# Four small reorderings in a fused attention and MLP kernel: memory read-out ahead, weight loads split, w_down scaling in segment 0, other LN times

## The chip, the cores and the metric

The kernel runs on one core of one Trainium2 chip. The metric is the device time of one execution in microseconds. A ratio is the mean time of one kernel's fast runs over the mean of the other's fast runs of the same rounds, so it isn't quite the ratio of the medians that are quoted beside it. "Faster" and "same" are meant at 2%.

## The reference

One block on 2048 tokens of width 448: an adaptive layer norm (LN) with modulation from `c`, attention in four segments of 512 tokens with a running memory `M`, a residual, a second adaptive LN, and a gated MLP.

```
mod = (silu(c) @ w_mod)                    # six rows: sa, ca, ga, sb, cb, gb
h = layernorm(x) * (1 + ca) + sa
for s in range(4):                         # segments of 512 tokens, 16 heads of 28
    a_dot = softmax(mask(q_s k_s^T * scale)) @ v_s
    a_mem = (phi(q_s) @ M) / (phi(q_s) @ z + 1e-6)      # phi(t) = t+1 if t>0 else exp(t)
    o_s   = g * a_mem + (1 - g) * a_dot
    M, z  = M + phi(k_s)^T @ v_s, z + sum(phi(k_s))
x = x + ga * (concat(o) @ wo)
h = layernorm(x) * (1 + cb) + sb
x = x + gb * ((sigmoid(h @ w_gate) * (h @ w_up)) @ w_down)
```

## The kernel before

The program is one list of jobs. Between the logits groups of a segment it takes jobs from a queue `fill`: projections of the next segments, the memory update, the output projection `wo_tile`, the MLP of the segment before. `later(ns, ...)` puts an instruction into the streams when the program's own reckoning of time has passed by so much. All DMA transposes and nearly all loads are issued by one engine, SyncE (SP).

The memory update. `pk` is phi(k), transposed by DMA; it has one buffer, so the `pk` of segment 1 can't be written before the `dM` matmuls of segment 0 have read theirs:

```python
def mem_k(s, hc):
    if hc == 0:
        pk_of[s] = pipe.tile([P, NHC, TPS, P], BF16, tag="pk", bufs=1, name="pk")
    pk = pk_of[s]
    phi(kT_of[s][:, hc, :], 3500, ("pk", s), lambda e: nc.sync.dma_start_transpose(pk[:, hc, :, :], e[:]))

def mem_update(s):
    ...
    for hc in range(NHC):
        for kb in range(TPS):
            nc.tensor.matmul(dMv[:, hc, :, :], lhsT=pk[:, hc, kb, :], rhs=vt_all[s][...], ...)
```

The attention output of a unit (segment, four heads) and its transposition, which the output projection waits for:

```python
def pv(s, hc):
    ... acc matmuls (40) ...
    if s > 0:
        ... mem matmuls (4) ...
    ... r1, t1 from acc; r2, t2 from mem; ou = t1 + t2 ...        # all VectorE

def otr(s, hc):
    nc.sync.dma_start_transpose(oT_of[s][:, hc, :, :], ou[:].rearrange("p t h e -> p (t h e)"))
```

The scaling of the weights by the modulation rows, and the order of jobs and loads:

```python
def prep_b1():
    ga = mod_rep(2, 1.0, "ga")                     # 4 matmuls, a copy on ScalarE
    wm[4] = load_wm(nc.sync, 4)
    ... later: wo_sb *= ga
def prep_b2():
    mod_cols(((3, 2), (4, 3)))
    wm[5] = load_wm(nc.sync, 5)
def prep_b3():                                      # in the list of segment 1
    gb = mod_rep(5, 0.5, "gb")
    for fc in range(0, NFC, 2):                    # 7 multiplies on VectorE
        later(1700 * fc + 800, lambda fc=fc: scale_w(wd_sb, fc, gb), "wd")
...
early_loads = [load_wo, load x of segment 3, load_wm3] + w_gate in 4 pieces + w_up in 4 pieces
fill.extend(spread(... jobs of segments 0 and 1 ..., early_loads, 2))
...
fill.extend(spread(j2[:4] + m[0][1:] + j2[4:8] + [(2000, prep_b2)], w_down in 4 pieces, 2))
```

The softmax here doesn't subtract the row's maximum and nothing guards it: scores larger than these inputs give would overflow.

Of the kernel before, what the change touches and what calls it, by code (L numbers as in the profile page):

```python
# [13 lines left out]
P = 128  # L14
# [3 lines left out]
def kernel(  # L18
# [84 lines left out]
    def load_x(eng, t0, t1):  # L103
        eng.dma_start(x_sb[:, t0:t1, :], x_dram[t0 * P:t1 * P, :].rearrange("(t p) d -> p t d", p=P))

    load_x(nc.sync, 0, 2)
    load_x(nc.scalar, 2, 4)
    nc.sync.dma_start(c_col[:], c.rearrange("o (k p) -> p (o k)", p=KP))
    qT_of = [const.tile([P, NHC, L], BF16, name=f"qT{s}") for s in range(3)]
# [34 lines left out]
    for b in wm_bufs:  # L144
        nc.vector.memset(b[:, NK * D:], 0.0)
    load_w(nc.sync, wq_st, A_wq)
    load_w(nc.scalar, wk_st, A_wk)
    load_w(nc.sync, wv_sb, A_wv)
# [83 lines left out]
    def mod_rep(j, mul, name):  # L232
        rp = m_f32("rp")
        for k in range(NK):
            nc.tensor.matmul(rp[:, 0:D], lhsT=silu_bc[:, k, :], rhs=wm[j][:, k * D:(k + 1) * D],
                             start=(k == 0), stop=(k == NK - 1))
        rep = const.tile([P, D], BF16, name=name, tag="rep")
        nc.scalar.mul(rep[:], rp[:, 0:D], mul)
        return rep
# [60 lines left out]

    def ln1_start(s, by_pe=False):
        def start():
# [7 lines left out]
            if not by_pe:  # L310
                for kc in range(NK):
                    later(14500 + 500 * kc, lambda kc=kc: ln.modulate(kc, 0), tag)
        return (0, start)
# [43 lines left out]
    def phi(src, wait, tag, then=None):  # L357
        e = work.tile([P, L], BF16, tag="e", bufs=6, name="e")
        nc.scalar.activation(e[:], src, AF.Exp)

        def fin():
            r = work.tile([P, L], BF16, tag="r", bufs=2, name="r")
            nc.vector.tensor_scalar(r[:], src, 0.0, 1.0, op0=ALU.max, op1=ALU.add)
            nc.vector.tensor_tensor(e[:], e[:], r[:], ALU.min)
            if then:
                then(e)
        later(wait, fin, tag)
        return e
# [57 lines left out]
    def pv(s, hc):  # L426
# [6 lines left out]
        for qb in range(TPS):  # L433
            for hs in range(4):
                for kb in range(qb + 1):
                    c0 = OFF[kb] + (qb - kb) * P
                    nc.tensor.matmul(accv[:, qb, hs, 0:ME], lhsT=pT[:, hs, c0:c0 + P],  # L437
                                     rhs=vt[:, kb, hc * 4 + hs, 0:ME], start=(kb == 0), stop=(kb == qb))
        if s > 0:
            mem = m_f32("mem")  # L440
            memv = mem[:].rearrange("p (t h e) -> p t h e", h=4, e=HP)
            need(("pq", u), ("rm", s))
            pq = pq_of.pop(u)
            for qb in range(TPS):
                nc.tensor.matmul(memv[:, qb, :, 0:ME], lhsT=pq[:, qb * P:(qb + 1) * P], rhs=rm_of[s][:, hc, :, :],
                                 start=True, stop=True)
        ou = ou_bufs[(s * NHC + hc) % 2]
        ou_of[u] = ou
        cb = lambda i: coef[:, i:i + 1, hc * 4:(hc + 1) * 4].to_broadcast([P, TPS, 4])
        r1 = work.tile([P, TPS, 4], F32, tag="r1", bufs=2)  # L450
        nc.vector.tensor_tensor(r1[:], accv[:, :, :, Dh], cb(0), ALU.mult)
        nc.vector.reciprocal(r1[:], r1[:])

        def bc(r):
            return r[:].rearrange("p t (h o) -> p (t h) o", o=1).to_broadcast([P, TPS * 4, Dh])

        def num(a):
            return a[:].rearrange("p (th e) -> p th e", e=HP)[:, :, 0:Dh]

        ouv = ou[:].rearrange("p t h e -> p (t h) e")[:, :, 0:Dh]  # L460
        if s == 0:
            nc.vector.tensor_tensor(ouv, num(acc), bc(r1), ALU.mult)
            return
        t1 = work.tile([P, TPS * 4, Dh], F32, tag="t1", bufs=1)
        nc.vector.tensor_tensor(t1[:], num(acc), bc(r1), ALU.mult)  # L465
        r2 = work.tile([P, TPS, 4], F32, tag="r2", bufs=2)
        nc.vector.scalar_tensor_tensor(r2[:], memv[:, :, :, Dh], 1e-6, cb(1), op0=ALU.add, op1=ALU.mult)
        nc.vector.reciprocal(r2[:], r2[:])
        t2 = work.tile([P, TPS * 4, Dh], F32, tag="t2", bufs=1)
        nc.vector.tensor_tensor(t2[:], num(mem), bc(r2), ALU.mult)  # L470
        nc.vector.tensor_tensor(ouv, t1[:], t2[:], ALU.add)

# [99 lines left out]
    def prep_b1():  # L572
        ga = mod_rep(2, 1.0, "ga")
        wm[4] = load_wm(nc.sync, 4)
        for k in range(0, NK, 2):
            later(1500 * k + 800, lambda k=k: scale_w(wo_sb, k, ga), "wo")
# [5 lines left out]
    def prep_b2():  # L582
        mod_cols(((3, 2), (4, 3)))
        wm[5] = load_wm(nc.sync, 5)

    def prep_b3():
        gb = mod_rep(5, 0.5, "gb")
        for fc in range(0, NFC, 2):
            later(1700 * fc + 800, lambda fc=fc: scale_w(wd_sb, fc, gb), "wd")

# [14 lines left out]
    for t in range(TPS):  # L605
        ln0.stats(t)
        if t % 2:
            ln0.rstd(t - 1, t + 1)
        if t == 1:
            silu_ops()  # L610
    mod_cols(((0, 0), (1, 1)), False)
    warm_up(NWARM[1])
    pts = [m_bf16("lntr") for _ in range(NK)]
    for k in range(NK):
        pad_copy(nc.scalar, wq_sb, wq_st, k)
    for t in range(TPS):
        ln0.norm(t)
        if t == 1:
            for k in range(NK):
                pad_copy(nc.vector, wk_sb, wk_st, k)  # L620
            mod_evac(((0, 0), (1, 1)))
        for kc in range(NK):
            nc.tensor.transpose(pts[kc][:, t * P:(t + 1) * P], ln0.xn[:, t, kc * P:(kc + 1) * P], ident[:])
    for kc in range(NK):
        ln0.pe_evac(pts[kc], kc, 0)
    load_x(nc.sync, TPS, 2 * TPS)
    load_x(nc.sync, 2 * TPS, 3 * TPS)
# [14 lines left out]

    def load_wm3():
        wm[3] = load_wm(nc.sync, 3)

# [10 lines left out]
    def spread(jobs, steps, every):  # L656
        steps, res = list(steps), []
        for i, j in enumerate(jobs):
            res.append(j)
            if i % every == every - 1 and steps:  # L660
# [3 lines left out]

    early_loads = [load_wo, lambda: load_x(nc.sync, 3 * TPS, 4 * TPS), load_wm3] \
        + [piece(wg_sb, B_w_gate, k) for k in range(NK)] + [piece(wu_sb, B_w_up, k) for k in range(NK)]
    fill.extend(sp(load_bw2))
    fill.extend(spread(j0[3:6] + sp(late_consts) + j0[6:10] + [ln1_start(2)] + j0[10:] + ln1_pe_jobs(1) + m[0][0:1]
                       + j1[:8], early_loads, 2))
    fill.extend([ln1_start(3)] + m[1][0:1] + j1[8:] + [(1000, prep_b1)])  # L670
    fill.extend(spread(j2[:4] + m[0][1:] + j2[4:8] + [(2000, prep_b2)], [piece_wd(f, min(f + 4, NFC)) for f in range(0, NFC, 4)], 2))
    fill.extend(j2[8:] + m[1][1:])
    fill.extend(j3)

# [6 lines left out]
    for s in range(NSEG):  # L681
        for hc in range(NHC):
            prev = (s, hc - 1) if hc else (s - 1, NHC - 1)
            for g in range(3):
                if prev[0] >= 0 and g == 1:
                    pv(*prev)
                    tick(1100)
                logits(s, hc, g)
                tick(450)
                if s >= 1 and hc == 1 and g == 0:  # L690
# [12 lines left out]
                    else:  # L703
                        fill.extend(h2_jobs(s - 1) + gj[:1] + [(1000, prep_b3)] + m[2][0:1] + gj[1:5] + m[2][1:] + gj[5:])
                    pace[0] = (cost(fill) - KEEP[s] * GU) / (12 if s < 3 else 9)
# [4 lines left out]
                if prev[0] >= 0 and g == 2:  # L710
                    otr(*prev)
    last = NSEG - 1
    dj = down_jobs(last - 1)
    run_fill(2000)
    pv(last, NHC - 1)
# [42 lines left out]
```

## Time and profile before

| | before |
|---|---|
| median of the first three runs | 274.89 us (274.32 to 276.37) |
| span in the profile, mean granted clock | 275.1 us, 0.975 |
| first projection matmul starts | 14.77 us |
| last `dM` matmul of segment 0 starts | 53.16 us |
| last `oT` of segment 0 issued / first residual of segment 0 | 71.31 / 77.33 us |
| first gate/up product `fT` | 98.29 us |
| fourth residual of segment 1 / last `dps` matmul | 137.00 / 271.44 us |

The marks of the last five rows are starts of single instructions in the trace, counted from the span's start. The residual is the VectorE addition `x_sb<-pwo,x_sb`; it follows the output projection, which has to wait until the segment's four `oT` have landed. The lines of the profile are read in the prediction.

### The profile page before, as it was taken

Reading aid. Unit: us, or ns where it says so; the run is one execution under the profiler, and the core shown is the slowest. Engines: PE = TensorE matmul, PEld = TensorE weight load, DVE = VectorE, ACT = ScalarE, POOL = GpSimd, SP = SyncE. Lnnn points to the kernel's source line nnn. Section 1 sums busy time; section 2 is a strip of 40 time slices with the busy share of each in tenths; the row PEclk is TensorE's granted clock in tenths of the full one; section 3 lists DMA queues with packets and bytes.
Section 4 is the critical chain, followed back from the end, with each engine's and each line's share of the span. In section 5 each row is a group of like instructions: output and inputs, shape, how many; then the busy total and the mean of one; then the engine's idle time right before and its main releaser. Section 6 shows DMA issues by size and latency. Waiting matters only on the chain.

```text
span 275.1 us, 5225 instructions
## 1 busy us (share of the span) xinstructions
PE 246.6 (90%) x2029; PEld 114.7 (42%) x2054; DVE 185.0 (67%) x429; ACT 139.2 (51%) x171; POOL 69.6 (25%) x130
## 2 busy tenths in 40 slices
PE   7599798896788689889989989999999999999995
PEld 2344444553343334444344443535443445433352
DVE  4569799944378748897995665797774669434421
ACT  1268489774727578666622767653564220033300
POOL 4109421450424312114351222224220004000000
PEclk9979799997979999999999999999999999999999
DMA  5999539488911100220031100003120001400001
GB/s 144 263 235 284 113 64 221 70 147 142 245 40 39 42 19 0 60 57 21 19 76 35 38 19 21 1 21 84 28 55 20 21 0 42 94 9 0 0 26 43
DMA packets 40960, 19.66 MB, mean 71 GB/s; under 512 B 29672, under 2 KB 40040, under 8 KB 40936
## 3 DMA queue, kind: packets, MB, share of 16 engines
q1 hardware_dynamic: 39720, 18.30, 30.8%
q10 hardware_dynamic: 1216, 1.03, 1.4%
q8 instruction: 16, 0.26, 0.5%
q14 instruction: 8, 0.07, 0.1%
HBM read 10.67 MB, written 1.84 MB: 45 GB/s over the span
## 4 chain that ended last, share of the span: by engine, by line
PE 44%; DVE 20%; DMA 6%; ACT 3%; issue 3%; SPq 1%; POOL 1%; DVEq 0%; ACTq 0%
PE ups L521 12%; PE dps L530 11%; PE gps L509 10%; PE gps L514 4%; DMA hT<-xn 3%; DVE st L257 3%; PE lg L412 2%; DVE x_sb L489 2%; PE acc L437 2%; DVE fT L524 2%; ACT pT L415 2%; DMA oT<-ou 2%; PE pwo L486 2%; DMA pk<-e 2%; DVE t L470 1%
## 5 line engine op out<-in xcount | busy, mean ns | idle before, releaser
L415 ACT ACTIVATE pT<-lg 128x2048 bf16<-128x2048 f32 (+1 forms) x48 | 76.6, 1595 | 55.1 <-PE lg L412 55.0
L524 DVE SCALAR_TENSOR_TENSOR fT<-tt,ups 128x512 bf16<-128x512 f32 x56 | 36.8, 684 | 36.7 <-PE ups L521 28.5
L423 POOL TENSOR_SCALAR_AFFINE_SELECT pT<-pT 128x512 bf16<-128x512 bf16 x64 | 41.2, 662 | 67.7 <-ACT pT L415 67.7
L517 ACT ACTIVATE tt<-gps 128x512 f32<-128x512 f32 x56 | 30.3, 595 | 44.9 <-PE gps L514 44.9
L530 PE MATMUL dps<-wd_sb,fT 128*128 128x448 bf16 x224 | 43.7, 353 | 0.0
L509 PE MATMUL gps<-hT,wg_sb 128*128 128x512 bf16 x155 | 40.4, 380 | 1.0 <-DVE t L465 0.4
L521 PE MATMUL ups<-hT,wu_sb 128*128 128x512 bf16 x164 | 40.2, 381 | 0.5 <-issue 0.5
L530 PEld LDWEIGHTS <-fT 128*128 128x128 bf16 x224 | 21.5, 98 | 20.5 <-issue 0.6
L521 PEld LDWEIGHTS <-wu_sb 128*128 128x128 bf16 x168 | 14.1, 98 | 25.5 <-issue 12.3
L261 POOL TENSOR_SCALAR rs<-mv 128x1 f32<-128x1 f32 (+2 forms) x21 | 5.2, 248 | 75.9 <-DVE mv L258 75.9
L509 PEld LDWEIGHTS <-wg_sb 128*128 128x128 bf16 x168 | 15.2, 98 | 20.0 <-issue 2.7
L437 PEld LDWEIGHTS <-pT 128*128 128x128 bf16 x640 | 18.8, 97 | 5.9 <-issue 2.2
L337 PE MATMUL pq<-hT,wq_sb 128*128 128x512 bf16 x60 | 18.2, 406 | 3.2 <-DVE hT L296 1.9
L257 DVE BATCH_NORM_STATS2 st<-x_sb 128x6 f32<-128x448 bf16 x32 | 19.8, 617 | 1.8 <-DMA x_sb<-in_A_x_dram 1.3
L412 PE MATMUL lg<-qT,kT 28*128 28x512 bf16 (+3 forms) x256 | 17.7, 310 | 3.4 <-ACT pT L415 3.4
L437 PE MATMUL acc<-vt,pT 128*128 128x29 bf16 x640 | 19.0, 177 | 1.4 <-POOL pT L423 1.2
L514 PE MATMUL ups<-hT,wgu_sb 64*128 64x512 bf16 x56 | 18.0, 382 | 2.0 <-DVE t L470 1.1
L534 DVE TENSOR_TENSOR ot<-dps,x_sb 128x448 bf16<-128x448 f32 x16 | 9.8, 618 | 13.2 <-PE dps L530 10.7
L514 PE MATMUL gps<-hT,wgu_sb 64*128 64x512 bf16 x56 | 17.1, 381 | 1.6 <-DVE hT L278 1.3
L349 PE MATMUL pv<-wv_sb,hT 128*128 128x448 bf16 x64 | 14.6, 367 | 4.2 <-DVE kT L342 4.2
L337 PE MATMUL pq<-hT,wk_sb 128*128 128x512 bf16 x61 | 17.0, 394 | 1.0 <-ACT qT L340 0.7
L486 PE MATMUL pwo<-wo_sb,oT 128*128 128x448 bf16 x64 | 14.8, 366 | 2.2 <-DMA oT<-ou 2.1
(88 smaller groups left out, 261.9 us busy)
## 6 DMA issues: line engine op xcount, KB each, us to landing
wm<-in_w_mod_dram SPq DMA_DIRECT2D x5, 392.0 KB, 7.9
out_dram<-ot SPq DMA_DIRECT2D x16, 112.0 KB, 1.7
x_sb<-in_A_x_dram SPq DMA_DIRECT2D x3, 448.0 KB, 7.3
wg_sb<-in_B_w_gate_dram SPq DMA_DIRECT2D x3, 448.0 KB, 9.1
wu_sb<-in_B_w_up_dram SPq DMA_DIRECT2D x3, 448.0 KB, 3.9
wd_sb<-in_B_w_down_dram SPq DMA_DIRECT2D x3, 448.0 KB, 3.7
wm<-in_w_mod_dram ACTq DMA_DIRECT2D x1, 392.0 KB
wo_sb<-in_A_wo_dram SPq DMA_DIRECT2D x4, 98.0 KB
```

What stands on the lines that cost most here:

```text
L257: nc.vector.bn_stats(st[:], self.srcs[i])
L337: nc.tensor.matmul(pq[:, 0:L], lhsT=head_cols(w_sb, k, hc), rhs=h[:, k, :], start=(k == 0), stop=(k == NK - 1))
L412: nc.tensor.matmul(lg[:, hs, wid:wid + nq], lhsT=kT[r, hc, kb * P:(kb + 1) * P], rhs=qT[r, hc, kb * P:L], start=True, stop=True, tile_posi ...
L415: nc.scalar.activation(pT[:, :, w0:w0 + wid], lg[:, :, 0:wid], AF.Exp, scale=scale)
L423: nc.gpsimd.affine_select(out=blk, in_=blk, compare_op=ALU.is_ge, fill=0.0, base=0, pattern=[[0, 4], [1, P]], channel_multiplier=-1)
L437: nc.tensor.matmul(accv[:, qb, hs, 0:ME], lhsT=pT[:, hs, c0:c0 + P], rhs=vt[:, kb, hc * 4 + hs, 0:ME], start=(kb == 0), stop=(kb == qb))
L509: nc.tensor.matmul(g[:, 0:L], lhsT=wg_sb[:, k, f], rhs=h[:, k, :], start=(k == 0), stop=False)
L514: nc.tensor.matmul(dst[:, 0:L], lhsT=wgu_sb[r:r + LW, f], rhs=h[r:r + LW, 3, :], start=first, stop=not first, tile_position=(r, 0))
L517: nc.scalar.activation(tt[:], g[:, 0:L], AF.Tanh, scale=0.5)
L521: nc.tensor.matmul(u[:, 0:L], lhsT=wu_sb[:, k, f], rhs=h[:, k, :], start=False, stop=(k == 2))
L524: nc.vector.scalar_tensor_tensor(ft[:], tt[:], 1.0, u[:, 0:L], op0=ALU.add, op1=ALU.mult)
L530: nc.tensor.matmul(dp[:, 0:D], lhsT=fT_of[(s, fc)][:, t * P:(t + 1) * P], rhs=wd_sb[:, fc, :], start=(fc == 0), stop=(fc == NFC - 1))
```

## The change

The intent was to fill TensorE's gaps before 140 us. There are four parts and an adjusted job list: `c` and the halves of wq and wk are loaded in another order, over both queues; the four `mem` matmuls of a unit and their VectorE work go one logits group ahead of its `acc` matmuls; `gb` and the seven w_down scalings move from segment 1 to segment 0, which needs w_down early and puts w_up in its place in the stream of loads, and swaps w_mod loads 3 and 5; the modulates of two LNs get other times. To make room, the tile `e` goes from six buffers to five.

```diff
+    nc.scalar.dma_start(c_col[:], c.rearrange("o (k p) -> p (o k)", p=KP))
     load_x(nc.sync, 0, 2)
     load_x(nc.scalar, 2, 4)
-    nc.sync.dma_start(c_col[:], c.rearrange("o (k p) -> p (o k)", p=KP))
...
-    load_w(nc.sync, wq_st, A_wq)
-    load_w(nc.scalar, wk_st, A_wk)
+    for st, w in ((wq_st, A_wq), (wk_st, A_wk)):
+        nc.sync.dma_start(st[:, 0:2, :], w[0:2 * P, :].rearrange("(k p) n -> p k n", p=P))
+        nc.scalar.dma_start(st[:, 2, :], w[2 * P:3 * P, :])
+        nc.scalar.dma_start(st[0:LW, 3, :], w[3 * P:D, :])
... (SiLU after all statistics; copies of wq after the transposes, of wk after the modulates)
-    later(14500 + 500 * kc, lambda kc=kc: ln.modulate(kc, 0), tag)
+    later(mod_at + 500 * kc, lambda kc=kc: ln.modulate(kc, 0), tag)
... (mod_at 14000 for segment 2, 19000 for segment 3; their starts moved)
-    e = work.tile([P, L], BF16, tag="e", bufs=6, name="e")
+    e = work.tile([P, L], BF16, tag="e", bufs=5, name="e")
... (mem matmuls, r2, t2 taken out of pv into mem_read; t2 has two buffers)
     def prep_b1():
         ga = mod_rep(2, 1.0, "ga")
         wm[4] = load_wm(nc.sync, 4)
+        gb = mod_rep(5, 0.5, "gb")
+        wm[3] = load_wm(nc.sync, 3)
+        for fc in range(0, NFC, 2):
+            later(8000 + 2000 * fc, lambda fc=fc: scale_w(wd_sb, fc, gb), "wd")
... (prep_b3 gone)
-    early_loads = [..., load_wm3] + w_gate pieces + w_up pieces
+    early_loads = [..., load_wm5] + w_down pieces + w_gate pieces + w_up pieces
...
-    fill.extend(spread(j2[:4] + m[0][1:] + j2[4:8] + [(2000, prep_b2)], [w_down pieces], 2))
+    fill.extend(spread(j2[:4] + m[0][1:] + j2[4:8] + [(2000, prep_b2)], early_loads[11:], 2))   # w_up
...
+                if prev[0] > 0 and g == 0:
+                    mem_read(*prev)
+                    tick(250)
```

More of the change, by code (lines that the diff above doesn't have):

```diff
@@ L236, in mod_rep @@
                              start=(k == 0), stop=(k == NK - 1))
-        rep = const.tile([P, D], BF16, name=name, tag="rep")
+        rep = const.tile([P, D], BF16, name=name)
         nc.scalar.mul(rep[:], rp[:, 0:D], mul)
@@ L299, with ln1_start @@
     ln1_of = {}
-    def ln1_start(s, by_pe=False):
+    def ln1_start(s, by_pe=False, mod_at=0):
         def start():
@@ L438, in pv @@
                                      rhs=vt[:, kb, hc * 4 + hs, 0:ME], start=(kb == 0), stop=(kb == qb))
-        if s > 0:
-            mem = m_f32("mem")
-            memv = mem[:].rearrange("p (t h e) -> p t h e", h=4, e=HP)
-            need(("pq", u), ("rm", s))
-            pq = pq_of.pop(u)
-            for qb in range(TPS):
-                nc.tensor.matmul(memv[:, qb, :, 0:ME], lhsT=pq[:, qb * P:(qb + 1) * P], rhs=rm_of[s][:, hc, :, :],
-                                 start=True, stop=True)
         ou = ou_bufs[(s * NHC + hc) % 2]
         ou_of[u] = ou
-        cb = lambda i: coef[:, i:i + 1, hc * 4:(hc + 1) * 4].to_broadcast([P, TPS, 4])
+        ouv = ou[:].rearrange("p t h e -> p (t h) e")[:, :, 0:Dh]
         r1 = work.tile([P, TPS, 4], F32, tag="r1", bufs=2)
-        nc.vector.tensor_tensor(r1[:], accv[:, :, :, Dh], cb(0), ALU.mult)
+        nc.vector.tensor_tensor(r1[:], accv[:, :, :, Dh], cb(0, hc), ALU.mult)
         nc.vector.reciprocal(r1[:], r1[:])
-        def bc(r):
-            return r[:].rearrange("p t (h o) -> p (t h) o", o=1).to_broadcast([P, TPS * 4, Dh])
-        def num(a):
-            return a[:].rearrange("p (th e) -> p th e", e=HP)[:, :, 0:Dh]
-        ouv = ou[:].rearrange("p t h e -> p (t h) e")[:, :, 0:Dh]
         if s == 0:
@@ L465, in pv, with mem_read, cb, bc @@
         nc.vector.tensor_tensor(t1[:], num(acc), bc(r1), ALU.mult)
+        nc.vector.tensor_tensor(ouv, t1[:], t2_of.pop(u)[:], ALU.add)
+    t2_of = {}
+    def mem_read(s, hc):
+        u = (s, hc)
+        mem = m_f32("mem")
+        memv = mem[:].rearrange("p (t h e) -> p t h e", h=4, e=HP)
+        need(("pq", u), ("rm", s))
+        pq = pq_of.pop(u)
+        for qb in range(TPS):
+            nc.tensor.matmul(memv[:, qb, :, 0:ME], lhsT=pq[:, qb * P:(qb + 1) * P], rhs=rm_of[s][:, hc, :, :],
+                             start=True, stop=True)
         r2 = work.tile([P, TPS, 4], F32, tag="r2", bufs=2)
-        nc.vector.scalar_tensor_tensor(r2[:], memv[:, :, :, Dh], 1e-6, cb(1), op0=ALU.add, op1=ALU.mult)
+        nc.vector.scalar_tensor_tensor(r2[:], memv[:, :, :, Dh], 1e-6, cb(1, hc), op0=ALU.add, op1=ALU.mult)
         nc.vector.reciprocal(r2[:], r2[:])
-        t2 = work.tile([P, TPS * 4, Dh], F32, tag="t2", bufs=1)
+        t2 = work.tile([P, TPS * 4, Dh], F32, tag="t2", bufs=2)
+        t2_of[u] = t2
         nc.vector.tensor_tensor(t2[:], num(mem), bc(r2), ALU.mult)
-        nc.vector.tensor_tensor(ouv, t1[:], t2[:], ALU.add)
+    def cb(i, hc):
+        return coef[:, i:i + 1, hc * 4:(hc + 1) * 4].to_broadcast([P, TPS, 4])
+    def bc(r):
+        return r[:].rearrange("p t (h o) -> p (t h) o", o=1).to_broadcast([P, TPS * 4, Dh])
+    def num(a):
+        return a[:].rearrange("p (th e) -> p th e", e=HP)[:, :, 0:Dh]
     def otr(s, hc):
@@ L583, in prep_b2 @@
         mod_cols(((3, 2), (4, 3)))
-        wm[5] = load_wm(nc.sync, 5)
-    def prep_b3():
-        gb = mod_rep(5, 0.5, "gb")
-        for fc in range(0, NFC, 2):
-            later(1700 * fc + 800, lambda fc=fc: scale_w(wd_sb, fc, gb), "wd")
     warm = ps_lg.tile([P, 4, 512], F32, tag="lg", name="warm")
@@ L608 @@
             ln0.rstd(t - 1, t + 1)
-        if t == 1:
-            silu_ops()
+    silu_ops()
     mod_cols(((0, 0), (1, 1)), False)
@@ L613 @@
     pts = [m_bf16("lntr") for _ in range(NK)]
-    for k in range(NK):
-        pad_copy(nc.scalar, wq_sb, wq_st, k)
     for t in range(TPS):
@@ L618 @@
         if t == 1:
-            for k in range(NK):
-                pad_copy(nc.vector, wk_sb, wk_st, k)
             mod_evac(((0, 0), (1, 1)))
@@ L623 @@
             nc.tensor.transpose(pts[kc][:, t * P:(t + 1) * P], ln0.xn[:, t, kc * P:(kc + 1) * P], ident[:])
+    for k in range(2):
+        pad_copy(nc.scalar, wq_sb, wq_st, k)
+        pad_copy(nc.vector, wq_sb, wq_st, 2 + k)
     for kc in range(NK):
         ln0.pe_evac(pts[kc], kc, 0)
+    for k in range(NK):
+        pad_copy(nc.vector, wk_sb, wk_st, k)
     load_x(nc.sync, TPS, 2 * TPS)
@@ L641, in load_bw2, with load_wm5 @@
         wm[2] = load_wm(nc.sync, 2)
-    def load_wm3():
-        wm[3] = load_wm(nc.sync, 3)
+    def load_wm5():
+        wm[5] = load_wm(nc.sync, 5)
     def piece(w_sb, w, k):
@@ L663, in spread @@
         return res
-    early_loads = [load_wo, lambda: load_x(nc.sync, 3 * TPS, 4 * TPS), load_wm3] \
-        + [piece(wg_sb, B_w_gate, k) for k in range(NK)] + [piece(wu_sb, B_w_up, k) for k in range(NK)]
+    early_loads = [load_wo, lambda: load_x(nc.sync, 3 * TPS, 4 * TPS), load_wm5] \
+        + [piece_wd(f, min(f + 4, NFC)) for f in range(0, NFC, 4)] + [piece(wg_sb, B_w_gate, k) for k in range(NK)] + [piece(wu_sb, B_w_up, k) for k in range(NK)]
     fill.extend(sp(load_bw2))
-    fill.extend(spread(j0[3:6] + sp(late_consts) + j0[6:10] + [ln1_start(2)] + j0[10:] + ln1_pe_jobs(1) + m[0][0:1]
-                       + j1[:8], early_loads, 2))
-    fill.extend([ln1_start(3)] + m[1][0:1] + j1[8:] + [(1000, prep_b1)])
-    fill.extend(spread(j2[:4] + m[0][1:] + j2[4:8] + [(2000, prep_b2)], [piece_wd(f, min(f + 4, NFC)) for f in range(0, NFC, 4)], 2))
-    fill.extend(j2[8:] + m[1][1:])
-    fill.extend(j3)
+    fill.extend(spread(j0[3:6] + sp(late_consts) + j0[6:8] + [ln1_start(2, mod_at=14000)] + j0[8:] + ln1_pe_jobs(1) + m[0][0:1]
+                       + j1[:8], early_loads[:11], 2))
+    fill.extend(j1[8:9] + [ln1_start(3, mod_at=19000)] + m[1][0:1] + j1[9:] + [(1800, prep_b1)])
+    fill.extend(spread(j2[:4] + m[0][1:] + j2[4:8] + [(2000, prep_b2)], early_loads[11:], 2))
+    fill.extend(j2[8:] + j3[:2] + m[1][1:] + j3[2:])
     def cost(jobs):
@@ L686 @@
                     pv(*prev)
-                    tick(1100)
+                    tick(1000)
                 logits(s, hc, g)
@@ L703 @@
                     else:
-                        fill.extend(h2_jobs(s - 1) + gj[:1] + [(1000, prep_b3)] + m[2][0:1] + gj[1:5] + m[2][1:] + gj[5:])
+                        fill.extend(h2_jobs(s - 1) + gj[:1] + m[2][0:1] + gj[1:5] + m[2][1:] + gj[5:])
                     pace[0] = (cost(fill) - KEEP[s] * GU) / (12 if s < 3 else 9)
@@ L711 @@
                     otr(*prev)
+                if prev[0] > 0 and g == 0:
+                    mem_read(*prev)
+                    tick(250)
     last = NSEG - 1
     dj = down_jobs(last - 1)
+    mem_read(last, NHC - 1)
     run_fill(2000)
```

## The prediction

> **What bounds the kernel now.** I read the busy page first, then one table of stages, then the waits, and last the timelines of VectorE and of the DMA-issuing queue around the two largest gaps. The page, columns being forty equal slices of the span:
>
> ```profile
> PE   7599798896788689889989989999999999999995
> DVE  4569799944378748897995665797774669434421
> PEclk9979799997979999999999999999999999999999
> ```
>
> Busy time by stage (columns: PE, weight load, DVE, ACT, POOL busy, then granted clock, DMA share, GB/s):
>
> ```profile
> 40.00:60.00 20.00, 18.16 (x225) 9.77 (x224) 17.08 (x43) 15.91 (x20) 7.51 (x11) 1.00 0.79 149
> 60.00:80.00 20.00, 14.84 (x147) 7.57 (x145) 8.38 (x20) 10.57 (x12) 4.61 (x8) 0.87 0.73 148
> 80.00:100.00 20.00, 15.99 (x149) 7.32 (x148) 15.83 (x42) 11.95 (x14) 6.87 (x13) 0.96 0.18 42
> 120.00:140.00 20.00, 17.89 (x163) 8.63 (x163) 18.20 (x42) 10.88 (x11) 7.19 (x14) 1.00 0.12 27
> 140.00:200.00 60.00, 58.26 (x518) 27.07 (x525) 43.02 (x96) 33.35 (x34) 16.16 (x30) 1.00 0.16 37
> ```
>
> So there are two kernels in one. From 140 us on TensorE is busy 97% (58.26 of 60) and only fewer matmuls would help. Before 140 us it is not full, and there the clock is low too: the page shows four dips of PEclk, the stage 60 to 80 was granted 0.87. What ends TensorE's gaps, in the waits of PE:
>
> ```profile
> PE pv L349 <- DVE kT L342: 4.2, 2, 2.8
> PE cp L218 <- DMA wm<-in_w_mod_dram: 2.2, 1, 2.2
> PE pwo L486 <- DMA oT<-ou: 2.1, 1, 2.1
> PE pq L337 <- DVE hT L296: 1.9, 2, 1.6
> PE ups L514 <- DVE t L470: 1.1, 3, 0.6
> ```
>
> The first is a queue effect. In VectorE's timeline the cast that TensorE waited for stands behind a modulate that waits for a DMA:
>
> ```profile
> 57.34 0.68 DVE L342 CAST kT<-pq 128x512 bf16<-128x512 f32 x1
> 63.13 0.73 DVE L278 TENSOR_SCALAR hT<-hT,cols 128x512 bf16<-128x512 bf16 x2 [5.12 <-DMA hT<-xn]
> 63.79 0.68 DVE L342 CAST kT<-pq 128x512 bf16<-128x512 f32 x1
> ```
>
> That DMA is late because the issuing queue (SP) is itself full, as its timeline shows (start, length):
>
> ```profile
> 47.05 1.25 SPq L477 DMA_TRANSPOSE oT<-ou  x1
> 48.39 6.21 SPq L374 DMA_TRANSPOSE pk<-e  x2
> 54.65 0.58 SPq L117 DMA_DIRECT2D wm<-in_w_mod_dram  x1
> 55.34 2.50 SPq L274 DMA_TRANSPOSE hT<-xn  x2
> ...
> 65.08 1.22 SPq L374 DMA_TRANSPOSE pk<-e  x1
> 66.35 3.07 SPq L654 DMA_DIRECT2D wd_sb<-in_B_w_down_dram  x3
> 69.52 0.41 SPq L117 DMA_DIRECT2D wm<-in_w_mod_dram  x1
> 70.03 2.55 SPq L477 DMA_TRANSPOSE oT<-ou  x2
> ```
>
> From 36.0 to 72.6 us SP has no pause: a transpose costs it about 1.2 us, a load 0.4 to 0.6. The second pk of 48.39 waits for the update matmuls dM of segment 0 (they end at 53.4) because pk has one buffer. The last oT is issued at 71.31 behind a burst of w_down loads and lands 5.57 us later in the chain of waits, where a transpose on a quiet queue takes 2.3. So between 53 and 77 us the path is dM, SP, DMA, not TensorE. From 77.33 to 97 the chain is VectorE: residual, statistics, the two read-out chains, normalise, transpose, modulate.
>
> **What the Trainium skill says.** "TensorE: Matmul & The Clock Gate", Part 1: after about one idle window of 3.4 us the array's clock halves, and a busy window releases it. The trace agrees: projection matmuls start every 0.43 us at 14.8 us and every 0.22 us at 19.5. The same page (spec table) calls VectorE a strict FIFO; the 5.12 us above, with a ready cast behind it, agrees. "DMA: Bandwidth & Descriptors", section "Issuing engines are not separate DMA queues": loads from two queues run on the same 16 engines and only issue time is saved. So I give the wq/wk split no bandwidth, only another order of landing; the DMA row, busy at 99% to 113% from 10 to 30 us by the stage table, fits that.
>
> **The change, part by part** (signs: minus is time won; the order of instructions on each engine of both kernels was compared).
>
> *Start.* Before, the DVE order put four wk copies, which waited for wk until 11.87 us, ahead of normalising tiles 2 and 3 (12.88). Now wq lands first, wk copies follow the modulates. The matrix of 392 KB less ahead of wq, at some 265 GB/s (slice GB/s), is 1.5 us earlier. Chain: modulation columns evacuated about 11.9, two normalises 0.7, last transposes to 13.3, first modulate 0.53, first projection at 13.85 instead of 14.77: -0.9. The wait for w_mod (2.2) stays; both w_mod loads remain ahead.
>
> *Segment 1's start.* All four statistics of segment 2, before three, now precede the transposed LN's modulates (29.28): one more statistics pair is 0.62 + 0.10 = +0.7, on the path, and the wait of 1.6 grows.
>
> *40 to 53 us.* Modulates of segment 2 move ahead of its last statistics: the waits of projections on them (gaps 47.14 to 47.76 and 48.09 to 49.14) go, -1.2. The gb row (four matmuls, 0.93 of PE) fills a gap in which TensorE waited for an exponential (0.83), but its 0.55 copy on ACT delays the next exponential, +0.6. With -0.2 carried in, dM of segment 0 ends about 0.8 earlier.
>
> *53 to 77 us.* From dM to the last oT SP issues 4 pk, 4 hT, 3 oT and 6 loads in both kernels. Hence the gap of 2.81 at 61.7 goes (segment 3's modulates now stand behind the casts), but TensorE then arrives early and waits for pk (dM of segment 1) and oT: the gap moves. What is truly won is SP's 0.8 plus a smoother burst: three w_up loads interleaved with pk, and no w_mod load at the end. Estimate: last oT lands about 73.4 instead of 76.9. After segment 3's hT (about 61) come five transposes at about 1.2 us and four loads, 1.57 MB in all, at some 330 GB/s (the fullest slices of the DMA view): 6.0 + 4.8, and about 1.6 of landing. That is -3.5.
>
> *77 to 97 us.* VectorE-bound. Three of the seven w_down scalings (0.54 to 0.62 each) land here, +1.6, and a third cast; of these about 1.1 fit in its waits (1.68 on hT, 0.46 on rs). The split of the read-out releases its PSUM tile before the other, and the last modulate precedes only the 1.05 us memory chain, not the whole 2.8 us: about -0.5. Net 0, so gate/up starts about 3.5 earlier.
>
> *97 to 140 us.* Removed from VectorE: seven scalings, 4.4. Removed from PE: gb's four matmuls. Read-out: reciprocal, scale and multiply of memory (0.16 + 0.25 + 0.62 = 1.05) now run while the 40 acc matmuls (about 1.0) do; the PSUM tile that "ups" waits for is free 1 us earlier. Gaps that should go, from PE's timeline: 107.4 (0.5), 118.2 (0.9), 130.8 (about 0.4); the two neighbouring logits groups at 109.8 now have a gate/up between, 1.35; the late mask at 138.8 (1.3) perhaps by 1. Sum -4.2. No instruction is removed in total; all is moved.
>
> *After 140 us.* Only the gap at 215.7 (0.5): -0.5.
>
> Sum: -3.5 - 4.2 - 0.5 = -8.2. Such sums overstate, since a removed gap lets the next wait show; I take some 85%: -6.9, so 268.0.
>
> **Rivals.** (1) *The gap only moves.* SP has the same number of issues between dM and oT, and e has five buffers for six. If the last oT still lands near 76, the first -3.5 shrinks to -1 and the total is 270.5 to 271.5: within 2%. For it: SP without pause for 36 us, DMA share 0.73 in 60 to 80. Against it: hT of segment 2 is normalised some 3 us earlier, so SP starts earlier. (2) *VectorE becomes the bound in 77 to 97.* It is already the chain there; if scalings and the third cast don't fit in its waits, +1.6: about 269.6. (3) *The clock.* Any new gap of 3 us can cost 1.7 us at half clock (3.4 us times one half); two fewer dips instead would win more, down to 265. (4) *Everything before 140 is hidden by TensorE's total.* Against: its work after 140 is dense in either kernel, so what is won before carries through.
>
> **Range and chances.** 268.0 with a spread of about 3 from rivals 1 and 2 downwards and 3 upwards: 264.5 to 272.5. The 2% line is 269.4; my point lies 1.4 below it, so 0.65 for faster, 0.33 for the same. Slower by 2% would need a new wait of 12 us: 0.02.
>
> **What would show it.** First projection near 13.9 us. No PE wait on the kT cast, but one on pk or oT between 65 and 75. Last oT of segment 0 landing at 72 to 75. First gate/up about 3 us earlier. "ups <- DVE t" gone from PE's waits, and PE busier than 18.5 of 20 in 100 to 120. After 140 us the same length to within 1 us. The prediction is wrong if the gap at 61.7 comes back whole at dM or oT, or if VectorE's share in 77 to 97 is full and gate/up starts no earlier.

## The result, and the profile after

The changed kernel takes 271.95 us (median of 4 runs, 271.51 to 272.43), the kernel before 275.63 (4 runs, 274.32 to 276.41). The ratio is 0.9872, 95% interval [0.9822, 0.9921]: the same at 2%, and about half of the gain that was forecast. The time lies inside the range of the prediction, near its upper end, and the likelier class was missed.

One caution for all comparisons with the trace of before: its run took 276.8 us, about 1.5 us over the kernel's median. The changed kernel's trace is of a run of 272.43 us, 0.5 over its median. The difference of these two traces overstates what was won by 0.7 us (4.4 for 3.7).

The page of the changed kernel, in forty slices:

```profile
PE   7599799889488789899999989999999999999995
PEclk9899799988979999999999999999999999999999
```

TensorE's row shows the weak place near 65 to 75 us again, now in one slice (the eleventh digit, a 4; before, the tenth and eleventh were 6 and 7), and PEclk still has four dips. The stages (same columns as in the prediction):

```profile
60.00:80.00 20.00, 15.53 (x163) 8.18 (x164) 9.78 (x24) 10.37 (x12) 5.19 (x9) 0.85 0.75 121
...
120.00:140.00 20.00, 18.73 (x184) 9.47 (x185) 17.26 (x43) 11.74 (x11) 7.98 (x16) 1.00 0.22 40
140.00:200.00 60.00, 58.50 (x529) 27.54 (x535) 41.90 (x96) 33.49 (x36) 15.96 (x28) 1.00 0.15 35
```

From 140 us on little changed, as it should be (58.50 of 60 us busy, before 58.26). The stage 120 to 140 is fuller (18.73 for 17.89). The stage 60 to 80, for which a large part of the gain was forecast, has 15.53 us busy, before 14.84; its clock is 0.85, before 0.87. The waits of TensorE tell why (line waited for, us, times, longest):

```profile
PE lg L414 <- ACT pT L417: 3.6, 6, 1.1
...
PE pwo L494 <- DMA oT<-ou: 2.6, 1, 2.6
PE cp L220 <- DVE silu L183: 2.4, 1, 2.4
PE dM L387 <- DMA pk<-e: 1.6, 1, 1.6
```

The projection's wait of 4.2 us on the cast `kT` is down to 0.3, but 1.6 us on `pk` are new and the wait on `oT` is 2.6 (2.1 before). SP's timeline of the changed kernel:

```profile
44.06 8.63 SPq L376 DMA_TRANSPOSE pk<-e  x2
...
60.45 2.63 SPq L485 DMA_TRANSPOSE oT<-ou  x1
63.12 0.58 SPq L656 DMA_DIRECT2D wu_sb<-in_B_w_up_dram  x1
63.80 1.19 SPq L376 DMA_TRANSPOSE pk<-e  x1
65.03 0.58 SPq L656 DMA_DIRECT2D wu_sb<-in_B_w_up_dram  x1
65.71 1.19 SPq L376 DMA_TRANSPOSE pk<-e  x1
66.94 0.58 SPq L656 DMA_DIRECT2D wu_sb<-in_B_w_up_dram  x1
67.57 0.48 SPq L655 DMA_DIRECT2D wgu_sb<-in_B_w_up_dram  x1
68.14 2.52 SPq L485 DMA_TRANSPOSE oT<-ou  x2
```

And what SP itself waited for:

```profile
SPq L376 <- PE dM L387: 4.1, 1, 4.1
```

The first of these lines holds two transposes of about 1.2 us each in 8.63 us. The rest is SP standing still from 45.3 to 51.5 us. It arrives at the first `pk` of segment 1 4.3 us earlier than before, and what ends this pause is `dM` of segment 0 releasing the single buffer (4.1 of the 6.2 us are put down to it). Before, the pause was shorter, 49.61 to 53.41 us. From 51.5 us on SP has two `wm` loads, four `hT`, three `pk`, four w_up loads and three `oT` to issue.

### The profile page after: what moved, and what is told of

Its sections match the earlier page's. It is cut to its first block, busy times and chain, and to the rows that moved or that the text cites. A ratio compares the mean times of both kernels' runs of the same rounds, so it can differ in the third digit from the quotient of the medians.

```text
span 270.7 us, 5234 instructions
## 1 busy us (share of the span) xinstructions
PE 245.1 (91%) x2029; PEld 115.4 (43%) x2054; DVE 184.1 (68%) x431; ACT 137.7 (51%) x169; POOL 70.0 (26%) x130
## 4 chain that ended last, share of the span: by engine, by line
PE 62%; DVE 16%; DMA 9%; ACT 7%; issue 4%; SPq 1%; POOL 1%; ACTq 0%; DVEq 0%
PE dps L538 15%; PE ups L529 13%; PE gps L517 12%; PE pq L339 6%; PE gps L522 5%; DMA wm<-in_w_mod_dram 4%; ACT pT L417 4%; PE lg L414 3%; PE acc L439 3%; DMA hT<-xn 3%; PE pwo L494 2%; DVE st L259 2%; DMA oT<-ou 2%; DVE xn L267 2%; DVE x_sb L497 1%
## 5 line engine op out<-in xcount | busy, mean ns | idle before, releaser
L542 DVE TENSOR_TENSOR ot<-dps,x_sb 128x448 bf16<-128x448 f32 x16 | 9.8, 620 | 13.0 <-PE dps L538 10.8
L267 DVE TENSOR_SCALAR xn<-x_sb,mv,rs 128x448 bf16<-128x448 bf16 x32 | 15.4, 498 | 0.4 <-POOL rs L264 0.4
```

## The experiments

Twelve kernels ran, all with a correct result. One small table tells the story of the stretch that the prediction staked most on: when the last `dM` matmul of segment 0 starts, how long from there to the issue of the last `oT` (the queue), how long from that to the first residual (the landing), and the ratio of the whole kernel to the kernel before.

| kernel | last dM(0) | + queue | + landing | first residual | ratio [95%] |
|---|---|---|---|---|---|
| before | 53.16 | 18.15 | 6.02 | 77.33 | 1 |
| changed | 51.25 | 18.20 | 6.57 | 76.02 | 0.9872 [0.9822, 0.9921] |
| start_only | 51.22 | 17.14 | 5.77 | 74.13 | 0.9896 [0.9856, 0.9936] |
| no_mem_ahead | 50.46 | 17.57 | 6.22 | 74.25 | 0.9858 [0.9826, 0.9890] |
| ln_times_old | 50.65 | 17.79 | 6.89 | 75.33 | 0.9872 [0.9828, 0.9915] |
| wd_late | 48.88 | 18.03 | 6.67 | 73.58 | 0.9920 [0.9891, 0.9950] |
| wup_late | 49.55 | 15.92 | 4.63 | 70.10 | 0.9683 [0.9652, 0.9714] |
| wup_late_tiny4 | 51.18 | 17.34 | 3.03 | 71.55 | 0.9767 [0.9738, 0.9797] |
| wup_act | 50.78 | 17.03 | 4.84 | 72.65 | 0.9786 [0.9745, 0.9826] |
| pk2 | 49.55 | 14.54 | 4.83 | 68.92 | 0.9675 [0.9645, 0.9706] |
| before_pk2 | 52.83 | 14.84 | 5.55 | 73.22 | 0.9915 [0.9880, 0.9950] |
| wup_late_tiny | 50.53 | 21.18 | 2.89 | 74.60 | 0.9869 [0.9833, 0.9905] |
| pk2_wup_late_th | 51.58 | 12.68 | 4.86 | 69.12 | 0.9666 [0.9617, 0.9714] |
| pk2_no_mem | 50.27 | 14.66 | 4.93 | 69.86 | 0.9738 [0.9704, 0.9773] |

The first column differs by 1.7 us between changed and pk2, which have the same start, because the clock dips before 35 us in the one trace and not in the other. The two middle columns are free of these early dips. They aren't free of later ones: every trace with one `pk` buffer has a dip that starts between 58 and 75 us, none of the four with two has. Each row is one trace, so tenths of a microsecond shouldn't be read from it.

**The start alone (start_only).** The kernel before with the new order of the first loads, SiLU and weight copies, and nothing else (the diff is the first part of the change).

> The kernel before with only the new start: c first on the ACT queue, wq and wk split over both queues, SiLU after all statistics, wq and wk copies after the normalises. Theory (the start is what shortened the stretch to 77 us): first projection near 12.9 us as in the changed kernel (before: 14.77), first residual of segment 0 at about 76.0 to 76.4 (before 77.33), ratio to before 0.993 to 0.996. Rival (the start's gain is absorbed by later waits, and the load order and LN times did it): first projection as early, but the first residual at 77.0 to 77.5 and a ratio of 0.998 or more.

The median is 273.04 us. The first projection starts at 12.32 us, the first residual at 74.13, earlier than in the full change (76.02). From the first residual to the fourth of segment 1 it needs 59.5 us, as the kernel before does (59.7); the full change needs 57.6. Both the ratio and the first residual are better than the ranges of either theory. By the ratios the start alone carries most of the net gain (the intervals overlap), and in these traces the rest of the change loses in the stretch what it wins behind it.

**Read-out back behind (no_mem_ahead).** The changed kernel, with the `mem` matmuls, r2 and t2 back in `pv`.

```diff
-                if prev[0] > 0 and g == 0:
-                    mem_read(*prev)
-                    tick(250)
...
+        if s > 0:
+            mem_mm(s, hc)              # in pv, after the acc matmuls
+        ... mem_dve(s, hc) after t1
```

> The changed kernel with the memory read-out put back behind the local part: its matmuls after the acc matmuls, its VectorE chain after the local one. Theory (the split frees the PSUM tile that ups waits for): the waits of ups on the memory multiply return (about 0.5 + 0.9 + 0.5 us), ratio to before about 0.993 instead of 0.987. Rival (the tile was free in time once the scalings of w_down had left VectorE): ratio 0.987 to 0.989, no such wait.

The median is 271.67 us, the ratio 0.9858, which the changed kernel's own interval covers; it is a little below the range of the rival too. The waits of `ups` on the memory multiply didn't return: 0.2 us in this trace, 1.1 before. So the rival fits, and the read-out ahead is worth nothing that can be measured here. The two intervals together leave room for some 1.6 us either way.

**Old LN times (ln_times_old).**

```diff
-    fill.extend(j1[8:9] + [ln1_start(3, mod_at=19000)] + m[1][0:1] + j1[9:] + [(1800, prep_b1)])
+    fill.extend([ln1_start(3)] + m[1][0:1] + j1[8:] + [(1800, prep_b1)])
     (segment 2 likewise; modulates at 14500 for both)
```

> The changed kernel with the LN times of before (both starts and the modulates at 14500). Theory (the 2.8 us wait on the kT cast only moved to pk and oT): the wait on the kT cast comes back, those on pk or oT shrink by as much, ratio to before 0.984 to 0.990. Rival (the LN times are worth that wait): 2 to 3 us slower than the changed kernel, ratio 0.995 to 0.999.

The median is 272.0 us. The wait on the cast `kT` is back and `dM` of segment 1 comes at 72.23 us instead of 68.18, yet the first residual is no later (75.33), and TensorE's waits on `pk` and `oT` are gone from its list. So removing that wait only let TensorE arrive sooner at the `oT` that weren't there.

**w_up after the stretch (wup_late).** The four w_up loads (3 of 448 KB, one of 224) are issued after the last `oT` of segment 0.

```diff
-    fill.extend(spread(j2[:4] + ... + [(2000, prep_b2)], early_loads[11:], 2))
+    fill.extend(spread(j2[:4] + ... + [(2000, prep_b2)], [], 2))
+                    if s == 1:
+                        fill.extend((0, f) for f in early_loads[11:])
```

> The changed kernel with the four w_up loads (1.57 MB) issued after the last oT transpose of segment 0 instead of before it. Theory (bytes in front of the transposes): at some 330 GB/s they are 4.8 us of the DMA engines, so the last oT lands some 3.5 to 4.5 us earlier than 75.6, the projection of outputs starts at about 72, and the ratio to before falls to 0.972 to 0.976. Rival 1 (issue time on SP): four issues of 0.57, so 2.3 us, ratio about 0.979. Rival 2 (VectorE or TensorE is the bound anyway): ratio 0.986 to 0.988.

266.91 us, more than the theory promised. SP's timeline of this kernel at the same place:

```profile
64.16 2.52 SPq L485 DMA_TRANSPOSE oT<-ou  x2
66.74 1.52 SPq L656 DMA_DIRECT2D wu_sb<-in_B_w_up_dram  x3
```

The queue is 2.3 us shorter and the landing 1.9. The gain is kept to the end: 5.9 us at the first residual, 5.4 at the last `dps`. So the four loads in the stretch cost the changed kernel some 5 us. They are no addition of the change, though: the kernel before issues four w_down loads there. No run took those out, so what they cost is not known.

**Bytes or issue time (wup_late_tiny, wup_late_tiny4, wup_act).** A load among the transposes can hurt in two ways: its 0.57 us on the queue, and its bytes on the 16 DMA engines. In wup_late_tiny four loads of 4 KB took the old places of the w_up loads.

```diff
+    scr = const.tile([P, H], BF16, name="scr")
+    def tiny():
+        nc.sync.dma_start(scr[:], A_beta.partition_broadcast(P))
```

> The w_up loads late as before, but in their old places on SP stand four loads of 4 KB each, so the number of issues ahead of the last oT is that of the changed kernel and only the bytes are gone. Theory (bytes): as good as the late loads alone, ratio 0.967 to 0.972. Rival (issue time on SP, 4 x 0.57 us): 2.3 us of the gain is lost again, ratio about 0.976.

271.75 us, ratio 0.9869, as slow as the full loads. This run doesn't decide: all four wrote one tile, so each waited for the one before to land (issues at 62.13, 64.92, 67.48 and 69.95 us). With a tile for each:

```diff
-    scr = const.tile([P, H], BF16, name="scr")
+    scr = [const.tile([P, H], BF16, name=f"scr{i}") for i in range(4)]
```

> As the earlier run with four 4 KB loads in the places of the four w_up loads (w_up itself issued after the last oT of segment 0), but each into a tile of its own, so that none waits for the one before. If the w_up loads hurt by their bytes (1.6 MB beside the transposes): as good as w_up late alone, ratio 0.967 to 0.971. If they hurt by the issue time on the queue (4 x 0.57 us = 2.3 us): first residual 72.3 instead of 70.1, ratio 0.975 to 0.979.

268.38 us, ratio 0.9767. And the other way round, meant to leave the bytes in place and take the issues off SP:

```diff
-        return lambda: nc.sync.dma_start(w_sb[:, k, :], ...)
+        return lambda: (nc.scalar if w_sb is wu_sb else nc.sync).dma_start(w_sb[:, k, :], ...)
```

> The changed kernel with the four w_up loads at the same places in the program but issued by ACT: same bytes in the same stretch, four issues fewer on SP. Theory (all bytes run on the same engines and must pass before the last oT): at most a small gain, ratio 0.982 to 0.988. Rival 1 (only what stands ahead in SP's own ring holds a transpose up): nearly the gain of the late loads, ratio 0.968 to 0.973. Rival 2 (issue time): 2.3 us, ratio about 0.979.

269.32 us, ratio 0.9786 (called unclear, as its interval crosses 0.98). This run doesn't separate the two either, because the bytes did not stay in place. The edit leaves the loads where they were in the program, but ScalarE hasn't SP's queue in front of them. The first and the last of the four in its timeline:

```profile
48.46 0.33 ACTq L656 DMA_DIRECT2D wu_sb<-in_B_w_up_dram  x1
...
62.26 0.49 ACTq L655 DMA_DIRECT2D wgu_sb<-in_B_w_up_dram  x1
```

In the changed kernel SP issues them from 63.12 to 67.57 us. Here three of them are issued by 53.97, and their bytes run beside `hT` of segment 3: the two `hT` issued at 53.51 and 54.81 land after 7.9 and 7.0 us. The last two `oT` land in 2.3 us.

What does separate the two is wup_late_tiny4, between the changed kernel and wup_late. In ratios, from 0.9872 to 0.9767 by taking the bytes away is 2.9 us, and from 0.9767 to 0.9683 by taking the four issues away too is 2.3 us, as much as four issues of 0.57. So both hurt, about equally; of the 2.9 up to 1.0 may be clock (see below). The bytes' part shows in the chain that ended last, as the time from the issue of the last `oT` to its landing, for the kernel before, the changed kernel and wup_late_tiny4:

```profile
71.31 5.57 DMA oT<-ou
```

```profile
69.45 6.12 DMA oT<-ou
```

```profile
68.52 2.58 DMA oT<-ou
```

**Two buffers for pk (pk2), on top of the change.** Room comes from the MLP's intermediate tiles, 14 instead of 16, and one t2 instead of two.

```diff
-            pk_of[s] = pipe.tile([P, NHC, TPS, P], BF16, tag="pk", bufs=1, name="pk")
+            pk_of[s] = pipe.tile([P, NHC, TPS, P], BF16, tag="pk", bufs=2, name="pk")
     (tag="fT", bufs=NFC; tag="t2", bufs=1)
```

> The changed kernel with two pk buffers instead of one (paid for by one t2 buffer less and two fT buffers less, which nothing should wait for). Theory (SP stands 6 us before the first pk of segment 1 because its buffer is read by dM of segment 0): that issue moves from 51.5 to about 47, the DMA chain to the last oT starts 3 to 4 us earlier, the first residual comes at 72 to 73.5, ratio 0.974 to 0.978. Rival (the normalised rows of segment 3 and the w_mod loads set the chain, not pk): the issue moves but the last oT lands within 1 us of 75.6, ratio 0.985 to 0.988.

266.68 us (265.86 to 267.42), ratio 0.9675: more than the theory promised. This version beats the kernel before by 3.3%, and the changed kernel by some 2.0% (not a clear 2%). Its page and SP's timeline:

```profile
PEclk9999999999999999999999999999999999999999
```

```profile
42.75 4.08 SPq L376 DMA_TRANSPOSE pk<-e  x2
46.92 1.06 SPq L117 DMA_DIRECT2D wm<-in_w_mod_dram  x2
48.09 3.23 SPq L276 DMA_TRANSPOSE hT<-xn  x2
...
62.75 2.56 SPq L485 DMA_TRANSPOSE oT<-ou  x2
```

SP goes from `pk` to `wm` to `hT` with little of the standstill left (the first line, 4.08 us, was 8.63 in the changed kernel). The same work, w_up loads included, is 5.4 us earlier (the last `oT` is issued at 64.09 us for 69.45), and in the profiled run the clock never dips.

**Both cures and an earlier table load (pk2_wup_late_th).** ScalarE's first tanh ahead of its weight issues, since TensorE's first modulation matmul now waits for it (the 2.4 us above).

```diff
-    nc.scalar.activation(th[:], c_col[:], AF.Tanh, scale=0.5)          # after the wq and wk issues
+    nc.scalar.activation(th[:], c_col[:], AF.Tanh, scale=0.5)          # before them
```

> Two pk buffers and the w_up loads late together, and the table load and tanh of c ahead of the wq and wk issues on ACT (in the changed kernel they stand behind an issue that waits until 7.4 us, and the modulation matmuls wait 2.4 us for SiLU). Theory: the two queue changes overlap almost wholly (each gives some 5.2 us, the pair 5.5 to 6.5 since TensorE is then the bound), and the start is 1 to 1.5 us earlier, of which most carries through: ratio 0.958 to 0.964. Rival (the queue changes add up): below 0.955. Rival (the start is absorbed): 0.966.

266.61 us, ratio 0.9666 [0.9617, 0.9714]: no better than pk2, as the rival (start absorbed) had it. The modulation matmuls start at 8.33 us, but the first projection at 13.10, later than pk2's 12.35; ScalarE issues its last piece of wq at 6.12 instead of 4.84 us. The last `dM` of segment 0 is 2.0 us later than pk2's, and the queue behind it 1.9 shorter, with no clock dip in either trace. So the earlier table load seems to have lost what the second cure won. Three things changed at once, and whether the two cures add is left open.

**Two buffers for pk in the kernel before (before_pk2).**

> The kernel before with nothing of the change in it, only two pk buffers instead of one (down-input tiles cut from 16 to 14 to make room). Theory A: the single pk buffer already set the 53 to 77 us stretch of the kernel before (its second pk issue waited from 48.4 to 53.4 us for dM of segment 0), so this alone wins about as much as it won on top of the change: first residual of segment 0 at 71 to 74 us instead of 77.3, ratio 0.978 to 0.985. Then the change's aim at this stretch missed the cause, which was there before. Rival B: the pk wait hurt only after the change, because of its load order (one w_mod load more in the stretch ahead of hT): ratio 0.995 to 1.005 and first residual near 77.

272.48 us, ratio 0.9915. The trace agrees with theory A (first residual 73.22, 4.1 earlier; 3.7 at the end), the times with neither: 2.3 us is less than A gives and more than B. Part of that is the long run (276.8 us) behind the trace of before. The two changes reinforce each other: the change alone wins 1.3%, pk2 alone 0.9%, both 3.3%, more than the intervals allow for a sum.

**w_down scaled late (wd_late).** `gb`, the seven scalings and the order of w_mod loads put back as before.

```diff
     def prep_b1():
-        gb = mod_rep(5, 0.5, "gb")
-        wm[3] = load_wm(nc.sync, 3)
-        ... later: wd_sb *= gb
+    def prep_b3():                      # in the list of segment 1
+        gb = mod_rep(5, 0.5, "gb")
+        ... later: wd_sb *= gb
```

> The changed kernel with gb and the seven w_down scalings put back into segment 1 (and the w_mod load order of the kernel before: load 3 early, load 5 after the modulation columns). Theory: taking the scalings out of segment 1 is what shortened 77 to 140 us by about 2, so here first residual to x_sb#8 is back to about 59.5 us from 57.6; on the other side one w_mod load of segment 3's stretch goes and the first residual comes earlier, 74 to 75 instead of 76.0. Together ratio 0.984 to 0.990, within noise of the changed kernel. Rival: the scalings were hidden in VectorE's waits: 77 to 140 stays at 57.6 and the ratio goes to 0.980 to 0.984 by the earlier start.

272.62 us, ratio 0.9920: outside what I expected (0.984 to 0.990), 1.3 us slower than the changed kernel by the ratios, with intervals that overlap. The traced run is the fastest of its six (271.58 us) and the changed kernel's the slowest of its four, so the traces put wd_late ahead where the times don't; only their parts can be used. The trace shows the two sides as expected: the first residual comes at 73.58 us, 2.4 earlier, and from there to the fourth residual of segment 1 it takes 59.05 us instead of 57.61. 1.4 of the 2.1 us that the change wins in that stretch come from this part (from the first `fT` on it is 38.17 for 36.51 us, 1.7, of which 0.2 is given back ahead of it).

**Two pk buffers without the read-out ahead (pk2_no_mem).**

> Two pk buffers, and the memory read-out back behind the local part. With the stretch 53 to 77 us freed, does the read-out ahead earn anything? My theory: still nothing, ratio within 0.003 of that of two pk buffers alone (0.9675). Rival: it was hidden by the later wait only, and is worth 1 us now: 0.971 or more.

267.53 us, ratio 0.9738 [0.9704, 0.9773], against pk2's 0.9675 [0.9645, 0.9706]. That is above what "nothing" allows and in the range of the rival. In the traces 0.8 of the difference is there at the first projection (13.18 against 12.35 us, a clock dip), and between the first residual and the first gate/up product it is 0.5 us (21.56 against 21.08), afterwards nearly none. So the read-out ahead may earn half a microsecond once the stretch is free; with intervals that touch, I leave it open.

**The clock, from all timed runs.** Each run reports its mean granted clock, and one window of 3.4 us at half clock lowers it by 0.0063 (3.4 times 0.5 over 270). The runs of one kernel differ by up to three such windows. Taking each kernel's own mean off, 109 runs of all kernels show 0.66 us per window (standard error 0.09; 0.64 without the one slow run). This is an association, as a run that waits longer may also have more windows. The changed kernel averaged 0.9775, pk2 0.9928: 2.4 windows, so by this estimate about 1.6 of the 5.3 us between them are clock and the rest is waits. The same estimate bears on the smaller differences: start_only, no_mem_ahead, wup_late_tiny4 and wup_late averaged 0.9855, 0.9873, 0.9870 and 0.9897, which is 0.8 to 1.3 us less of clock loss than the changed kernel.

## Why the prediction was wrong

Its steps against the two traces (the last dps matmul is the end used here):

| step | predicted | measured |
|---|---|---|
| first projection | -0.9 | -1.85 |
| segment 1's start | +0.7 | +0.66 (first acc at 32.10 for 33.29, so -1.19 left) |
| dM of segment 0 ends | -0.8 | -1.9 |
| 53 to 77 us: last oT lands, residual starts | -3.5 | -1.3 |
| 77 to 97 us | 0 | +0.1 |
| 97 to 140 us | -4.2 | -2.2 |
| after 140 us | -0.5 | -1.0 |
| sum | -8.2, taken as -6.9 | -4.4 in these traces, -3.7 by the medians |

**The step that failed first is "53 to 77 us", -3.5, and in it the last term of its sum: "about 1.6 of landing".** The prediction counted 6.0 us for five transposes and 4.8 for four loads from the end of segment 3's `hT` at about 61, and then 1.6 until the last `oT` has landed, at 73.4. In the trace `hT` ends at 60.4 and SP needs 10.3 us for the same nine issues, a little less than the 10.8. But the last `oT` then takes 4.9 us to land (70.67 to 75.58), not 1.6. In the kernel before, with as many loads just ahead, it was 4.3 (72.58 to 76.89); the prediction had counted the loads' bytes as moved by then. wup_late_tiny4 shows that it is the bytes: without them the same term is 1.4 us (69.74 to 71.10).

It foresaw rightly that the wait on the cast would move to `pk` and `oT`. It then credited the stretch from dM to the landing with 2.7 us beyond dM's own 0.8. The table of the experiments shows that the queue from dM to the last `oT` is as long as before (18.20 for 18.15 us) and the landing 0.55 longer: "a smoother burst: three w_up loads interleaved with pk" wasn't smoother. Two experiments on this stretch, w_up out of it and two buffers for pk, each win about 5 us, which is more than the step had promised. Rival (1) of the prediction, the gap only moves, put the total at 270.5 to 271.5, and 271.95 was measured.

**What SP gained before dM was lost in a standstill.** The change gets `hT` of segment 2 onto the queue at 30.5 us instead of 36.0. The prediction named this as an argument against rival (1). But the single pk buffer holds SP until dM of segment 0 has run, and dM stands in TensorE's own order; so SP waited 4.1 us for it. The prediction showed the buffer's wait in the trace of before (48.39, 6.21) but read SP as without pause from 36.0 to 72.6 us; 3.8 us of that (49.61 to 53.41) were already a standstill. It didn't ask what an earlier SP would meet there. That two buffers are worth more with the change than without fits this: the standstill before dM is 3.8 us without and 6.2 with it.

**The second step that failed is "97 to 140 us", -4.2; it measured -2.2.** The mechanism of the scalings was right, only the size was off: wd_late puts 1.7 of the 2.2 us down to them and gb, where 4.4 us of VectorE work had been taken out. The read-out, which was to free the tile for `ups`, wasn't needed for it: without it (no_mem_ahead) that wait is 0.2 us, for 1.1 before. The rest was a list of gaps to disappear. Those at 107.4, 109.8 and 118.2 us did, but others of the same kind came. In the timeline of TensorE before, gb's matmuls stood between two logits groups:

```profile
98.77 0.29 PE L412 MATMUL lg<-qT,kT 28*128 28x256 bf16 x4
98.99 0.93 PE L235 MATMUL rp<-wm,silu_bc 112*128 112x448 bf16 x4
```

After, the second logits group waits for the exponential of the first, here and again at 114 us:

```profile
97.59 0.29 PE L414 MATMUL lg<-qT,kT 28*128 28x256 bf16 x4
99.01 0.40 PE L414 MATMUL lg<-qT,kT 28*128 28x512 bf16 x4 [1.13 <-ACT pT L417]
...
114.41 0.40 PE L414 MATMUL lg<-qT,kT 28*128 28x384 bf16 x8 [0.73 <-ACT pT L417]
```

In the waits over 97 to 140 us, those on the exponential rose from 1.8 to 2.3 us. The prediction counted the gap at 109.8 as gone and didn't look for the place that gb's matmuls would leave bare. wd_late, where gb's matmuls stand between those two groups again (95.15 us), has the short wait there (0.26 us) and the 1.13 at a later pair, at 107.35. No run moved gb's matmuls alone.

**What was right.** The start, with its sign and more than its size: the transposes no longer wait 0.89 us for the modulation columns, and the modulation matmuls start 0.7 earlier. Segment 1's +0.7: among the traces without an early clock dip, ln_times_old takes 17.33 us from the first projection to the first acc, and wd_late, wup_late and pk2, with the new times, 17.89 to 18.05. The net 0 in 77 to 97 us, though no run tells its terms apart. PE busy in 100 to 120 us (18.66 of 20), and the wait of `ups` on `t` gone. After 140 us no change beyond about a microsecond. The wait for w_mod, however, didn't "stay": it became a wait of 2.4 us for SiLU. The discount of 15% for "the next wait shows" was the right idea at the wrong place: it should have applied whole to the step whose next wait was already named. The clock rival was real too, as the estimate above shows, but it didn't favour the changed kernel: both profiles have four dips. What the prediction cites for the clock, a halving after one idle window, its trace shows only in part: the two rates of the matmuls agree, but in the 3.4 us before each of the four dips of the kernel before TensorE was busy for 1.65, 1.83, 0.77 and 1.44 us. (Two small slips change nothing: 0.16 + 0.25 + 0.62 is 1.03, not 1.05, and the DMA row from 10 to 30 us is 113% and 108%.)

Open: whether the read-out earns anything, what the five buffers of `e` cost (not tested alone), what the w_down loads cost the kernel before, and why before_pk2's times show less than its trace.

## What to carry to other kernels

When a queue is full, an instruction moved ahead on it wins little until the slowest gate behind it (here one buffer and the matmuls that free it) moves too: follow the queue from that gate, count what stands between the gate and the transfer that the next engine waits for, the landing included, and move other loads out of there. On top of the change, two buffers for a tile that crosses two engines and a DMA, or four loads issued later, were each worth more than the whole change. And when instructions are taken out of a place, look at what they had been covering.

## What the Trainium skill lacked or had wrong

- "DMA: Bandwidth & Descriptors", section "Issuing engines are not separate DMA queues", says that issuing from several engines only saves issue time, "which is usually small relative to the DMA itself". That holds of one load here (0.57 us of issue, 6.7 to landing), but misleads on a full queue: four loads of 4 KB on SP's queue cost 2.3 us of the kernel (wup_late_tiny4 against wup_late), some 4 x 0.57. And another issuer changed more than issue time: the first w_up load left ScalarE at 48.46 us, SP at 63.12.
- The same page, section "DMA Transpose (X-bar)", lists constraints but not what a transpose costs the issuing queue, and no page has it for such a tile (a table in its trn3 part has cycles for other sizes). Here it is 1.2 us for a 128 x 512 tile, two to three times a load's 0.41 to 0.58; and the median landing of the three `oT` of the stretch is 3.0 us with little else in flight, 6.1 beside 1.6 MB of loads.
- "TensorE: Matmul & The Clock Gate", section "Terms", puts the penalty of throttled time at about that time times (1 - K/N), from which a window of 3.4 us at half clock is an estimated 1.7 us. Over 109 runs such a window went with 0.66 us of the kernel's time (standard error 0.09), presumably because TensorE isn't the bound in all of it. That windows differ from run to run of one kernel, as Part 1 says, agrees: pk2's runs had a mean clock from 0.985 to 1.0.
